# A filter loaded twice by two queues, one product moved to GpSimd, and a shifted schedule in the setup of a fused FFT filter and feed-forward kernel

## The chip, the cores and the metric

The kernel runs on one core of one Trainium2 chip. The metric is device time in microseconds (us), the median of several executions. In this kernel TensorE (PE) multiplies matrices, VectorE (DVE) and ScalarE (ACT) do element-wise work, and GpSimd (POOL) does some of it, more slowly: a two-input operation on 128x512 takes 1.27 us there (L596 on the page of the kernel before) and 0.69 us on VectorE (L591). GpSimd issues DMAs through a software queue (q0 of that page, 13.60 MB), SyncE (SP) through a hardware queue (q1, 73.81 MB), and ScalarE through a hardware queue of its own (q10, 0.13 MB). The page gives the time of all queues as shares of the same 16 DMA engines (10.5%, 32.0% and under 0.1%).

## The reference

```python
# x (8, 3008, 256) f32; filt_r, filt_i (1505, 256); w_in (256, 2048); w_out (2048, 256); beta (2048,)
X = np.fft.rfft(x, axis=1)
y = np.fft.irfft(X * (filt_r + 1j * filt_i)[None], n=3008, axis=1)   # float32
h = y.reshape(-1, 256) @ w_in
out = (h / (1 + np.exp(-beta * h))) @ w_out
```

## The kernel before

The Fourier transform is done as matrix products in four small steps. Batch 0 is transformed in a setup of some 36 us. After that TensorE alternates between feed-forward products (`hps`, `acc`) and the transform steps of the next batch, for all eight batches. In the setup the filters arrive in six units of four rows. A product needs a unit's filter on all 128 partitions, but each DMA fills only 64 of them (`fr` the upper half, `fi` the lower), and GpSimd copies it into the other half:

```python
def load_filters(k0, k1):                     # SyncE: each filter to one half only
    for filt, dst, p0 in ((filt_r, fr_sb, M), (filt_i, fi_sb, 0)):
        for q0, off, sg in ((p0, k0, 1), (p0 + H, N1 - k0, -1)):
            ...
            nc.sync.dma_start(dst[q0 : q0 + H, k0:k1, :], src)

def spread(u):                                # GpSimd: copy to the other half
    nc.gpsimd.tensor_copy(fr_sb[:M, ks, :], fr_sb[M:, ks, :])
    nc.gpsimd.tensor_copy(fi_sb[M:, ks, :], fi_sb[:M, ks, :])

def s2_0(u):                                  # second transform step, times the filter
    ... # four matmuls into ps
    nc.vector.tensor_tensor(pq[u, 0][:], ps[:], fr_sb[:, ks, :], ALU.mult)
    nc.vector.scalar_tensor_tensor(pq[u, 1][:], ps[:], rot[:], fi_sb[:, ks, :], ALU.mult, ALU.mult)

for u in range(4):
    spread(u)
load_win(0, 4 * P)       # GpSimd: 0.26 MB of w_in
spread(4)
load_win(4 * P, FF)      # 0.79 MB of w_in
spread(5)
for g in range(4):
    load_x(1, g)         # GpSimd: xg, the input of batch 1
load_wout(0)             # SyncE: the first half of w_out, two loads of 0.52 MB
load_wout(WG)
scale_wout(0)            # GpSimd
scale_wout(WG)
```

In the trace GpSimd's instructions come in the order of this listing: the copies of unit 3 at 21.32 and 22.41 us, the first part of w_in at 23.40, the copies of unit 4 from 24.29, the second part at 26.37, the copies of unit 5 from 27.14, xg from 29.21, the scaling from 31.34. `unit(u)` is the third transform step of a unit (TensorE, with an evacuation on ScalarE), `a0_turn` transposes, and `spin` is a few matmuls that only keep TensorE busy.

Of the kernel before, what the change touches and what calls it, by code (L numbers as in the profile page):

```python
# [10 lines left out]
P = 128  # L11

ACT = mybir.ActivationFunctionType
ALU = mybir.AluOpType
ENG = mybir.EngineType
F32 = mybir.dt.float32
# [5 lines left out]
N1 = 47  # L22
M = 64
H = M // 2
NK = 24
# [11 lines left out]
def kernel(  # L37
# [10 lines left out]
    nc = tc.nc  # L48

    B, S, D = x.shape  # L50
# [27 lines left out]
    fr_sb = consts.tile([P, NK, D], F32, name="fr_sb", tag="fr_sb")  # L78
    fi_sb = consts.tile([P, NK, D], F32, name="fi_sb", tag="fi_sb")
    KH = 8  # L80
    KU = 4
# [1 line left out]
    WZ = KP * J  # L83
    CH = M * J

    def load_filters(k0, k1):
        n = k1 - k0
        for filt, dst, p0 in ((filt_r, fr_sb, M), (filt_i, fi_sb, 0)):
            for q0, off, sg in ((p0, k0, 1), (p0 + H, N1 - k0, -1)):
                src = AP(filt.tensor, filt.offset + off * D, [[N1 * D, H], [sg * D, n], [1, D]])  # L90
                nc.sync.dma_start(dst[q0 : q0 + H, k0:k1, :], src)  # L91

    t1 = consts.tile([NP, KP], BF16, name="t1", tag="t1")
    t4 = consts.tile([KP, NP], BF16, name="t4", tag="t4")
# [37 lines left out]
    def bank2(shape, dt=F32):  # L132
        return spsum.tile(shape, dt, name="sps", tag="sps")

    def turn8():
        return tpsum.tile([P, KH, P], BF16, name="tps", tag="tps")
# [20 lines left out]
    sr = rpool("setup_a", r_sr, bufs=1)  # L157
# [59 lines left out]
    off = affine("off", c_i, -TURN / 4, TURN / 4)  # L217
# [49 lines left out]
    def spin(n, idle):  # L267
        for _ in range(n):
            nc.tensor.matmul(idle[:], lhsT=rest[:, :P], rhs=rest[:], start=True, stop=True)

    def a0_turn(u, tiles=None, engines=(True,)):
        tiles = tiles or [turn8()]
        n = KU // len(tiles)
        for h, tp in enumerate(tiles):
            for i in range(n):
                k4 = 4 * (u * KU + h * n + i)
                for e in range(NDC):
                    nc.tensor.transpose(
                        tp[:, NDC * i + e, :],
                        aT[:, e, k4 : k4 + 4, :].rearrange("p c j -> p (c j)"),  # L280
                        ident[:],
                    )
        for h, tp in enumerate(tiles):
            k0 = u * KU + h * n
            dst = a0[:, k0 : k0 + n, :].rearrange("p k (e d) -> p (k e) d", e=NDC)
            evac(dst, tp[:, : NDC * n, :], engines[h])
# [7 lines left out]
    def t3_neg(g, on_act):  # L294
        ks = slice(g * KH, (g + 1) * KH)
        evac(t3[:, ks, P:], t3[:, ks, :M], on_act, -1.0)
# [12 lines left out]
    seen = sp.tile([1, 2], BF16, name="seen", tag="seen")  # L309
    nc.sync.dma_start(seen[:], t2[:1, 1, M - 2 : M])  # L310
    for u in range(NUN):
        load_filters(u * KU, (u + 1) * KU)
    gp = nc.gpsimd
    rot = affine("rot", v_i, 2.0, -1.0, gp)
    tiny = sp.tile([P, NFB], F32, name="tiny", tag="tiny")
# [19 lines left out]
    spin(2, idle)  # L335
    s1_0(7, (False, True))
    spin(2, idle)
    a0_turn(0, [turn8(), bank2([P, KH, P], BF16)], (False, True))
    a0_turn(1)
    t3_neg(0, False)  # L340
    nc.vector.reciprocal(rbeta_sb[:], beta_sb[:])

# [14 lines left out]
    WG = 4  # L357
    wstage = {}

    def load_x(b, g):  # L360
        t = xpool.tile([KP, JG, D], BF16, name="xg", tag="xg")
        load_rows(t[:], b, g * JG, (g + 1) * JG)
        xg[b, g] = t
# [9 lines left out]
    def scale_wout(f0):  # L373
        nc.gpsimd.tensor_tensor(
            wout_sb[:, f0 : f0 + WG, :],
            wstage.pop(f0)[:],
            rbeta_sb[:, f0 : f0 + WG].unsqueeze(2).broadcast_to([P, WG, D]),
            ALU.mult,
        )
# [42 lines left out]
    pq = {}  # L422
    r_p0 = ExitStack()
    p0pool = rpool("p0pool", r_p0, bufs=2, **tw)

    def s2_0(u):
        ps = bank2([P, KU, D])
        for i in range(KU):
            k1 = u * KU + i
            nc.tensor.matmul(ps[:, i, :], lhsT=t2[:, k1, :], rhs=a0[:, k1, :], start=True, stop=True)  # L430
        ks = slice(u * KU, (u + 1) * KU)
        for c in range(2):
            pq[u, c] = p0pool.tile([P, KU, D], BF16, name="pq_t", tag=f"pq{c}")
        nc.vector.tensor_tensor(pq[u, 0][:], ps[:], fr_sb[:, ks, :], ALU.mult)
        nc.vector.scalar_tensor_tensor(
            pq[u, 1][:], ps[:], rot[:], fi_sb[:, ks, :], ALU.mult, ALU.mult
        )
# [21 lines left out]
    def unit(u):  # L459
        t = bank2([P, NDC, KU, P])  # L460
        s3_0(u, [t[:, e] for e in range(NDC)])
        ck = KU * P // J
        dst = zT[:].rearrange("p e (j k) -> p e j k", k=KP)
        evac(
            dst[:, :, :, u * ck : (u + 1) * ck],
            t[:].rearrange("p e k (c j) -> p e j (k c)", j=J),
            True,
        )

    def spread(u):  # L470
        ks = slice(u * KU, (u + 1) * KU)
        nc.gpsimd.tensor_copy(fr_sb[:M, ks, :], fr_sb[M:, ks, :])  # L472
        nc.gpsimd.tensor_copy(fi_sb[M:, ks, :], fi_sb[:M, ks, :])  # L473
# [6 lines left out]
    for u in range(4):  # L480
        spread(u)
    load_win(0, 4 * P)
    spread(4)
    load_win(4 * P, FF)
    spread(5)
    for g in range(4):
        load_x(1, g)
    load_wout(0)
    load_wout(WG)
    scale_wout(0)  # L490
    scale_wout(WG)

    s2_0(0)
    a0_turn(2)
# [3 lines left out]
    unit(0)  # L498
    a0_turn(3)
    s2_0(2)  # L500
    unit(1)
    a0_turn(4)
    s2_0(3)
    unit(2)
    s2_0(4)
    a0_turn(5)
    t3_part(2, True)
    t3_neg(2, True)
    unit(3)
    s2_0(5)  # L510
    idle = tpsum.tile([P, 512], F32, name="tps", tag="tps")
    spin(3, idle)
    unit(4)
    banks.close()

# [14 lines left out]
    for e in range(NDC):  # L530
        for h in range(2):
            pool, tag = (lps, "lp") if e else (fps, "fp")
            ps = pool.tile([P, 4, P], F32, name="fp", tag=tag)
# [117 lines left out]
    def at(s, fn, *a):  # L651
        plan.setdefault(int(s), []).append((fn, a))

    def s1_steps(b, units_, steps, act, on_act=()):
        assert len(steps) == len(units_)
        for i, s in zip(units_, steps):
            at(s, s1, b, i, i in on_act)
            if i % 4 == 3:
                at(s, a1_store, b, i // 4)
# [12 lines left out]
    for b in range(1, B):  # L672
        o = first_step[b - 1]
        if b == 1:
            at(0, z_late, 1, 0)
            at(1, z_late, 1, 1)
            s1_steps(1, range(16), [1 + (2 * i + 1) // 3 for i in range(16)], False, (1, 4, 7, 10, 13))
            for i, r in enumerate((11, 12, 13, 14)):
                at(r, f_late, 1, i // 2, i % 2)
            for g in range(NG):  # L680
                at(o + 13, a2_load, 1, g)
            for hh, z0, f0 in ((2, (13, 14), (15, 16, 17, 18)), (3, (18, 19), (20, 21, 22, 23))):
                for e in range(NDC):
                    at(z0[e], z_late, hh, e)
                for i, r in enumerate(f0):
                    at(r, f_late, hh, i // 2, i % 2)
            s23_steps(1, [o + r for r in (22, 24, 26, 28, 30, 34, 36, 38, 40, 42, 44, 46)], 5, 1)
            for h in range(J // JG):
                at(o + 54, zz_load, 1, h)
            s4_steps(1, [o + 66 + (i * 12) // 15 for i in range(16)], 2)  # L690
            for f in (2, 3):
                at(f, load_wout, f * WG)
                at(f, scale_wout, f * WG)
            if B > 2:
                for g in range(4):
                    at(o + 24 + 3 * g, load_x, 2, g)
                late = (54, 55, 56, 57, 58, 59, 60, 61, 66, 67, 68, 70, 72, 73, 74, 76)
                s1_steps(2, range(16), [o + r for r in late], False)
                for g in range(NG):
                    at(o + 80, a2_load, 2, g)  # L700
                if B > 3:
                    for g in range(4):
                        at(o + (62, 68, 88, 92)[g], load_x, 3, g)
            continue
        base = [o + 16 * n + s for n in range(4) for s in (4, 8, 12)]
        if b == 2:
            base[:6] = [o + r for r in (8, 12, 19, 22, 26, 29)]
        s23_steps(b, base, 6, False)
        for h in range(J // JG):
            at(o + 70, zz_load, b, h)  # L710
        s4_steps(b, [o + 80 + (i * 13) // 15 for i in range(16)], False)
        if b + 1 < B:
            early = [o + 16 * n + s for n in range(4) for s in (7, 13)]
            late = [o + s for s in (66, 67, 69, 70, 72, 73, 75, 76)]
            s1_steps(b + 1, range(16), early + late, False)
            for g in range(NG):
                at(o + 82, a2_load, b + 1, g)
            if b + 2 < B:
                for g in range(4):
                    at(o + (30, 62, 88, 92)[g], load_x, b + 2, g)  # L720
# [6 lines left out]
    for s in range(NSTEP):  # L727
        i, fb = divmod(s, NFB)
# [100 lines left out]
```

## Time and profile before

| | before |
|---|---|
| time, median of 3 runs | 782.0 us |
| span of the profiled run | 780.25 us |
| last unit of filters landed | about 26.7 us |
| second part of w_in issued, landed | 26.37, 34.73 us |
| first xg issued, landed | 29.21, 36.56 us |
| first matmul on xg (the rest of the program follows without a wait) | 36.61 us |

The table gives instants from the start of the span, read from the trace's instructions and DMA landings. From the first xg matmul to the end are 780.25 - 36.61 = 743.6 us. The prediction below shows the lines that matter. In them `sps` and `lp` are results of the second and third transform steps, `pq_t` the products with the filters, `y`, `zz`, `zp` and `fp` stages behind them, `ws` w_out as it lands and `wout_sb` the same scaled.

### The profile page before, as it was taken

To read this page: it belongs to the slowest core of one execution; us is meant where nothing else is said; L and a number is where in the kernel's file an instruction comes from. 1 tells how busy PE (TensorE), PEld (TensorE's weight loads), DVE (VectorE), ACT (ScalarE), POOL (GpSimd) and SP (SyncE) were. 2 spreads that over 40 slices of the span, in tenths; PEclk is the share of its full clock that TensorE was granted. 3 is DMA by queue.
4 is the path that set the end of the run, shared out by engine and by line. 5 is a ranking of instruction groups with operands and counts; after the bars stand their busy time and mean duration, and the time that the engine had idled before them with its cause. 6 is when DMAs were issued, how large, how long until landed. Compare 5 with 4: busy or idle time off the path is not lost.

```text
span 780.2 us, 15154 instructions
## 1 busy us (share of the span) xinstructions
PE 764.1 (98%) x5956; PEld 544.0 (70%) x6051; DVE 446.0 (57%) x713; ACT 552.6 (71%) x814; POOL 151.4 (19%) x155
## 2 busy tenths in 40 slices
PE   8899999999999999999999999999999999999997
PEld 5677667766776667866678666776667776676665
DVE  7869754766556665566546665567655666321001
ACT  6767877676677766777667776677766777777776
POOL 6714400312012210122201322022200222000000
PEclk9999999999999999999999999999999999999999
DMA  9975585244913358042671417622164111500101
GB/s 185 233 213 116 147 209 155 70 108 115 252 42 80 103 116 242 29 113 71 152 207 45 119 48 181 176 75 69 48 189 135 48 48 49 156 28 28 55 28 55
DMA packets 84411, 88.51 MB, mean 113 GB/s; under 512 B 5788, under 2 KB 74652, under 8 KB 84340
## 3 DMA queue, kind: packets, MB, share of 16 engines
q1 hardware_dynamic: 79892, 73.81, 32.0%
q0 software_dynamic: 4304, 13.60, 10.5%
q8 instruction: 47, 0.77, 0.4%
q14 instruction: 24, 0.20, 0.1%
q10 hardware_dynamic: 144, 0.13, 0.0%
HBM read 54.47 MB, written 46.66 MB: 130 GB/s over the span
## 4 chain that ended last, share of the span: by engine, by line
PE 94%; DMA 2%; issue 1%; POOL 1%; DVE 1%; SPq 0%; ACT 0%; DVEq 0%; POOLq 0%
PE acc L788 43%; PE hps L770 39%; PE ps L561 3%; PE ps L629 3%; PE ps L607 3%; PE ps L577 2%; DMA xg<-in_x_dram 1%; DMA fi_sb<-in_filt_i_dram 1%; POOL fi_sb L473 0%; POOL fr_sb L472 0%; SPq L91 0%; PE ps L405 0%; PE tp L400 0%; DVE y L114 0%; DVE u L224 0%
## 5 line engine op out<-in xcount | busy, mean ns | idle before, releaser
L779 ACT ACTIVATE gT<-hps,beta_sb 128x512 bf16<-128x512 f32 x752 | 516.9, 687 | 213.3 <-PE hps L770 191.9
L788 PE MATMUL acc<-wout_sb,gT 128*128 128x256 bf16 x3008 | 452.9, 272 | 2.3
L770 PE MATMUL hps<-y,win_sb 128*128 128x512 bf16 (+7 forms) x1636 | 428.0, 350 | 0.1
L788 PEld LDWEIGHTS <-gT 128*128 128x128 bf16 x3008 | 286.9, 98 | 121.6 <-issue 0.9
L596 POOL TENSOR_TENSOR yh<-a_t,b_t 128x512 bf16<-128x512 f32 x84 | 106.4, 1267 | 424.1 <-DVE b_t L595 422.8
L770 PEld LDWEIGHTS <-win_sb 128*128 128x128 bf16 x1728 | 164.8, 98 | 25.2 <-issue 0.9
L112 DVE COPY ost<-acc 128x512 f32<-128x512 f32 (+1 forms) x94 | 59.9, 679 | 138.3 <-PE acc L788 138.2
L112 DVE CAST a<-ps 96x512 bf16<-96x512 f32 x107 | 72.9, 685 | 53.3 <-PE ps L561 49.3
L114 DVE TENSOR_SCALAR y<-ps 128x376 bf16<-128x376 f32 (+2 forms) x128 | 63.3, 510 | 61.2 <-PE ps L629 57.9
L591 DVE TENSOR_TENSOR a_t<-ps,fr_sb 128x512 f32<-128x512 f32 x84 | 58.1, 692 | 67.0 <-PE ps L577 66.5
L592 DVE SCALAR_TENSOR_TENSOR b_t<-ps,fi_sb 64x512 f32<-64x512 f32 x84 | 58.2, 693 | 1.1
L595 DVE TENSOR_TENSOR b_t<-ps,fi_sb 64x512 f32<-64x512 f32 x84 | 57.4, 683 | 1.1
L112 DVE CAST z<-ps 128x512 bf16<-128x512 f32 x72 | 49.3, 684 | 1.7 <-PE ps L607 0.8
L629 PEld LDWEIGHTS <-zz 96*128 96x128 bf16 x448 | 29.7, 97 | 22.9
L561 PE MATMUL ps<-xg,t 94*96 94x512 bf16 x112 | 41.9, 381 | 1.5 <-DMA xg<-in_x_dram 0.8
L629 PE MATMUL ps<-t,zz 96*128 96x94 bf16 x448 | 34.7, 205 | 0.7
L607 PE MATMUL ps<-yh,t 128*128 128x256 bf16 x168 | 32.1, 273 | 0.6
L577 PE MATMUL ps<-a,t 128*128 128x256 bf16 x168 | 32.1, 273 | 0.3
L607 PEld LDWEIGHTS <-t 128*128 128x128 bf16 x168 | 16.2, 98 | 17.7 <-issue 0.7
L577 PEld LDWEIGHTS <-t 128*128 128x128 bf16 x168 | 16.1, 98 | 16.3
L171 POOL DMA_DIRECT2D xg<-in_x_dram x24 | 12.5, 521 | 56.7 <-PE ps L561 56.7
L561 PEld LDWEIGHTS <-t 94*96 94x96 bf16 x112 | 13.8, 123 | 10.3
(95 smaller groups left out, 177.3 us busy)
## 6 DMA issues: line engine op xcount, KB each, us to landing
out_dram<-ost SPq DMA_DIRECT2D x42, 512.0 KB, 3.0
d<-a SPq DMA_DIRECT2D x28, 384.0 KB, 5.1
a<-d SPq DMA_DIRECT2D x28, 384.0 KB, 4.9
d<-z SPq DMA_DIRECT2D x28, 384.0 KB, 3.9
zz<-d SPq DMA_DIRECT2D x28, 384.0 KB, 7.1
xg<-in_x_dram POOLq DMA_DIRECT2D x24, 384.0 KB, 6.3
out_dram<-ost SPq DMA_DIRECT2D x9, 256.0 KB, 3.8
ws<-in_moe_w_out_dram SPq DMA_DIRECT2D x4, 512.0 KB, 6.6
```

What stands on the lines that cost most here:

```text
L112: nc.vector.tensor_copy(dst, src)
L114: nc.vector.tensor_scalar_mul(dst, src, scale)
L561: nc.tensor.matmul(ps[:KP], lhsT=t1[:], rhs=xg[b, g][:NP, jj : jj + 2, :], start=True, stop=True)
L577: nc.tensor.matmul(ps[:, e, :], lhsT=t2[:, k0 + e, :], rhs=st["a2", b, g][:, kk + e, :], start=True, stop=True,)
L591: nc.vector.tensor_tensor(a_t[:], ps[:], fr_sb[:, ks, :], ALU.mult)
L592: nc.vector.scalar_tensor_tensor(b_t[:M], ps[M:], -1.0, fi_sb[M:, ks, :], ALU.mult, ALU.mult)
L596: nc.gpsimd.tensor_tensor(yh[:], a_t[:], b_t[:], ALU.add)
L607: nc.tensor.matmul(ps[:, e, :], lhsT=t3[:, 2 * i + e, :P], rhs=yh[:, e, :], start=True, stop=True)
L629: nc.tensor.matmul(ps[:, e, :NP], lhsT=zz[:, j0 % JG + e, dc * P : (dc + 1) * P], rhs=t4[:], start=True, stop=True,)
L770: nc.tensor.matmul(hps[:, pos - t0 : pos - t0 + ln], lhsT=win_sb[:, dc, fb * P : (fb + 1) * P], rhs=ys[b][:, dc, n0 : n0 + ln], start=(dc ...
L779: nc.scalar.activation(gT[:], hps[:], ACT.Silu, scale=beta_sb[:, fb : fb + 1])
L788: nc.tensor.matmul(acc_of(i, tb)[:, tb % 2, :], lhsT=blk[i * NFB + fb][:, tb * P : (tb + 1) * P], rhs=wout_sb[:, fb, :], start=(fb == 0 an ...
```

## The change

The intent is to free GpSimd, which spends four copies of 1.04 us on the last two units, and with it the issue of w_in and xg. Units 4 and 5 are loaded into both halves, the second time by ScalarE's queue, so that one queue can fill one half while the other fills the other. One of the two products of unit 4 goes to GpSimd, from a copy that ScalarE makes and scales. Transposes and units are reordered, and the first transform of batch 1 starts one step later, with four late pieces of batch 0 moved to steps 2 to 5.

```diff
+    DUP = 2 * KH
+    def load_filter(i, k0, k1, p0, eng):  # one filter, either half, any queue
 ...
     for u in range(NUN):
-        load_filters(u * KU, (u + 1) * KU)
+        for i, p0 in enumerate((M, 0)):
+            load_filter(i, u * KU, (u + 1) * KU, p0, nc.sync)
 ...
+    load_filter(0, DUP, NK, 0, nc.scalar)
     a0_turn(0, ...)
     a0_turn(1)
+    load_filter(1, DUP, NK, M, nc.scalar)
 ...
+        if on_pool:
+            nc.scalar.activation(zc[:], ps[:], ACT.Copy, scale=rot[:])
         nc.vector.tensor_tensor(pq[u, 0][:], ps[:], fr_sb[:, ks, :], ALU.mult)
+        if on_pool:
+            return
 ...
     load_win(0, 4 * P)
-    spread(4)
     load_win(4 * P, FF)
-    spread(5)
-    for g in range(4):
-        load_x(1, g)
+    load_x(1, 0)
+    # pool_product(u): two GpSimd products of 128x512 from zc and fi_sb
 ...
     s2_0(2)
+    a0_turn(4)
     unit(1)
-    a0_turn(4)
     s2_0(3)
+    a0_turn(5)
+    s2_0(4, True)
+    pool_product(4)
+    for g in range(1, 4):
+        load_x(1, g)
+    scale_wout(0)
+    scale_wout(WG)
     unit(2)
 ...                       # unit(3) moves behind s2_0(5) and spin
-            s1_steps(1, range(16), [1 + (2 * i + 1) // 3 ...
-            for i, r in enumerate((11, 12, 13, 14)):
+            s1_steps(1, range(16), [2 + (2 * i + 1) // 3 ...
+            for i, r in enumerate((2, 3, 4, 5)):
                 at(r, f_late, 1, i // 2, i % 2)
```

More of the change, by code (lines that the diff above doesn't have):

```diff
@@ L84 @@
     CH = M * J
-    def load_filters(k0, k1):
-        n = k1 - k0
-        for filt, dst, p0 in ((filt_r, fr_sb, M), (filt_i, fi_sb, 0)):
-            for q0, off, sg in ((p0, k0, 1), (p0 + H, N1 - k0, -1)):
-                src = AP(filt.tensor, filt.offset + off * D, [[N1 * D, H], [sg * D, n], [1, D]])
-                nc.sync.dma_start(dst[q0 : q0 + H, k0:k1, :], src)
+    FILTERS = ((filt_r, fr_sb), (filt_i, fi_sb))
+    DUP = 2 * KH
+    def load_filter(i, k0, k1, p0, eng):
+        filt, dst = FILTERS[i]
+        for q0, off, sg in ((p0, k0, 1), (p0 + H, N1 - k0, -1)):
+            src = AP(filt.tensor, filt.offset + off * D, [[N1 * D, H], [sg * D, k1 - k0], [1, D]])
+            eng.dma_start(dst[q0 : q0 + H, k0:k1, :], src)
     t1 = consts.tile([NP, KP], BF16, name="t1", tag="t1")
@@ L424, with s2_0 @@
     p0pool = rpool("p0pool", r_p0, bufs=2, **tw)
-    def s2_0(u):
+    zc = sr.tile([P, KU, D], F32, name="zc", tag="zc")
+    def s2_0(u, on_pool=False):
         ps = bank2([P, KU, D])
@@ L482, with pool_product @@
     load_win(0, 4 * P)
-    spread(4)
     load_win(4 * P, FF)
-    spread(5)
-    for g in range(4):
-        load_x(1, g)
+    load_x(1, 0)
+    def pool_product(u):
+        for i in range(0, KU, 2):
+            k0 = u * KU + i
+            nc.gpsimd.tensor_tensor(
+                pq[u, 1][:, i : i + 2, :], zc[:, i : i + 2, :], fi_sb[:, k0 : k0 + 2, :], ALU.mult
+            )
     load_wout(0)
     load_wout(WG)
-    scale_wout(0)
-    scale_wout(WG)
     s2_0(0)
@@ L500 @@
     s2_0(2)
+    a0_turn(4)
     unit(1)
-    a0_turn(4)
     s2_0(3)
+    a0_turn(5)
[5 more added lines that the diff above has]
+    scale_wout(WG)
     unit(2)
-    s2_0(4)
-    a0_turn(5)
     t3_part(2, True)
     t3_neg(2, True)
-    unit(3)
     s2_0(5)
@@ L512 @@
     spin(3, idle)
+    unit(3)
     unit(4)
@@ L676 @@
             at(1, z_late, 1, 1)
-            s1_steps(1, range(16), [1 + (2 * i + 1) // 3 for i in range(16)], False, (1, 4, 7, 10, 13))
-            for i, r in enumerate((11, 12, 13, 14)):
+            s1_steps(1, range(16), [2 + (2 * i + 1) // 3 for i in range(16)], False, (1, 4, 7, 10, 13))
+            for i, r in enumerate((2, 3, 4, 5)):
                 at(r, f_late, 1, i // 2, i % 2)
             for g in range(NG):
-                at(o + 13, a2_load, 1, g)
+                at(o + 14, a2_load, 1, g)
             for hh, z0, f0 in ((2, (13, 14), (15, 16, 17, 18)), (3, (18, 19), (20, 21, 22, 23))):
```

## The prediction

> **What bounds the kernel now.** I read the page's busy times, then the waits of TensorE, the chain in order of time, the timelines of the engines and the DMA view by stretch. The page says TensorE is the bound of the whole:
>
> ```profile
> PE 764.1 (98%) x5956; PEld 544.0 (70%) x6051; DVE 446.0 (57%) x713; ACT 552.6 (71%) x814; POOL 151.4 (19%) x155
> ```
>
> The waits of TensorE from 28 us to the end name all that is left to win (us in total, times, longest):
>
> ```profile
> PE sps L444 <- ACT y L110: 1.1, 1, 1.1
> PE ps L561 <- DMA xg<-in_x_dram: 0.8, 1, 0.8
> PE lp L444 <- DVE pq_t L435: 0.6, 1, 0.6
> ```
>
> The reader is to see that nothing is listed after the wait for xg, which ends at 36.61 us: from there to 780.2 us TensorE never waits noticeably. The change leaves TensorE's work as it is. So the end is the start of the first matmul on xg (batch 1's first transform) plus a constant, and the whole question is what happens before 36.6 us. Even a setup of half the length would hardly be 2%.
>
> What sets that start? The chain in order of time, cut to its end (start, us, what):
>
> ```profile
> 22.41 0.93 POOL fi_sb L473
> ...
> 27.14 1.03 POOL fr_sb L472
> ...
> 28.23 0.39 POOL fi_sb L473
> 28.62 0.59 issue
> 29.21 7.35 DMA xg<-in_x_dram
> 36.56 0.04 issue
> 36.61 0.38 PE ps L561
> ```
>
> GpSimd's copies between the halves hold back the issue of xg, and xg then takes 7.35 us. That looks like an order to shorten GpSimd's list. The DMA views of two stretches, 11 to 24.7 us and 25 to 27.5 us, warn against it:
>
> ```profile
> DMA packets 2370, 3.22 MB, mean 235 GB/s; under 512 B 399, under 2 KB 1980, under 8 KB 2369
> DMA packets 795, 0.79 MB, mean 318 GB/s; under 512 B 19, under 2 KB 795, under 8 KB 795
> ```
>
> In both, the busy share of the 16 DMA engines is 9 in nearly every slice; page part 2 shows the same up to about 40 us. First x of batch 0, then 3.1 MB of filters (to 24.8 us), 1.05 MB of w_out, 1.05 MB of w_in and xg stand in one saturated line. xg takes 7.35 us because w_in is ahead of it, not because it was issued late.
>
> The third bound is VectorE's chain of products, one unit per 2.32 us (from its timeline: start, us, engine, line):
>
> ```profile
> 25.38 1.21 DVE L434 TENSOR_TENSOR pq_t<-sps,fr_sb 128x1024 bf16<-128x1024 f32 x1
> 26.52 1.27 DVE L435 SCALAR_TENSOR_TENSOR pq_t<-sps,rot,fi_sb 128x1024 bf16<-128x1024 f32 x1
> 28.20 1.22 DVE L434 TENSOR_TENSOR pq_t<-sps,fr_sb 128x1024 bf16<-128x1024 f32 x1 [0.41 <-POOL fr_sb L472]
> 29.34 1.27 DVE L435 SCALAR_TENSOR_TENSOR pq_t<-sps,rot,fi_sb 128x1024 bf16<-128x1024 f32 x1
> ```
>
> It ends at 30.61; the last unit waited 0.41 us for GpSimd's copy. From there the tail (last unit, turns, fourth transform) leads to the first hps matmul at 33.84.
>
> [...] filters, each to one half, 235 GB/s; w_out, over 128 partitions, 318. [...] from 36.5 to 40 us, with xg on one queue and w_out on the other, they moved 178 and 150 packets. [...] The trace's own row (L596, 128x512 from f32) has 1.27 us, which I use.
>
> **The change part by part.**
>
> GpSimd: four copies of units 4 and 5 go, 4 x 1.04 = 4.2 us. Two products of 128x512 come, 2 x 1.27 = 2.5 us. The w_in loads and the first xg load no longer have copies in between: were fi of unit 3 copied at 23.45 as now, xg's first load would be issued near 25.1 instead of 29.21.
>
> VectorE: one product of unit 4 goes, 1.14 us of its cadence, and with it the 0.41 us of waiting. Without any data wait it would end at 30.61 - 1.55 = 29.1.
>
> ScalarE: four DMA issues, by the SP queue's 0.4 us each 1.6 us, half of them before an evacuation that the first product needs (there ScalarE is idle 0.82 us, so nearly hidden); one scaled copy of 128x1024, 1.02 us; its slack of some 2 us between 21 and 28 us takes it.
>
> TensorE: the first xg matmul moves one step later, behind two more hps matmuls (0.43 us that then lies before the wait): -0.43 us if xg sets the time.
>
> DMA: two filters of 8 rows for 64 partitions, 2 x 64 x 8 x 1 KB = 1.05 MB more, in front of w_in and xg for the most part. Alone at 235 GB/s that is 4.5 us. If the second queue always met the other half, the two would run near the 318 GB/s of w_out or somewhat more. SP's queue changes halves every 262 KB, the ACT queue every 524 KB, so about half of the bytes meet the same half: 1.05 MB of SP's beside 1.05 MB of ACT's is then 1.05/0.36 + 1.05/0.225 = 7.6 us (estimate; 360 for opposite halves, because the fast 1 KB packets of this stretch take the same 46 ns as those of w_out and some are 4 KB) against 4.5 us for SP's alone. Delay of all that follows: 3.1 us. [...]
>
> So the last filters land near 26.7 + 3.1 = 29.8 us instead of about 26.7 (the next-to-last landing is at 26.1): the last product starts at about 29.8 and not at 28.0, and ends near 31.1. The products on GpSimd end near 30, so the fifth unit's second half and its evacuation come about when the last unit's do. The setup then ends 0.2 to 0.5 us later than now, in place of 1.5 earlier: the copies' time is given back as transfer time.
>
> xg: 36.56 + 3.1 for the filters, less what is taken from w_out, which now shares the DMA engines packet for packet with an earlier w_in: 250 to 2000 ns, say 1.2. That gives 38.5. The matmul starts 38.5 - 36.6 = 1.9 us later; less 0.43 makes +1.5 us.
>
> **The rivals.**
>
> A, the intended course: [...] the 1.05 MB cost only about 1 us; the setup ends 1 us or more earlier, w_in starts at 25.5 and xg lands at 36 or before. For it: most 4 KB filter packets take about 290 ns, a few 159[...]; and the moved steps (transform at step 2, four late pieces at steps 2 to 5) look fitted to a measured course. Against it: xg can't land before all the filters, w_in and itself have moved. It makes -1.5 to 0 us.
>
> B, full collision: the queues serialize [...], w_in isn't brought forward because GpSimd's copies of unit 3 wait for late filters, and the product on GpSimd comes last. For it: the saturated DMA row. It makes +2.5 to +4 us.
>
> C, a new wait after the first steps: w_out's first groups come later, and their scaling on GpSimd, now behind the products and three xg issues, must be ready for the first acc matmul (37.7 us now; scaling ended near 33.2, so 4.5 us of slack). I expect no wait, at most 1 us.
>
> **Range and chances.** My middle course says +1.5, A about -0.8, B +3. With weights 0.45, 0.4 and 0.15 the mean is 0.675 - 0.32 + 0.45 = +0.8; from 782.0 I choose 782.7. The range holds A whole and most of B: 780.3 to 785.2. 2% is 15.6 us, a good part of the whole setup of 36 us, so either side gets 0.01.
>
> **What would show each step right or wrong.** Right: a DMA queue of 1.05 MB on ScalarE; the throughput between 17 and 25 us only somewhat above 235 GB/s (260 to 300); VectorE's last product waits for a DMA and not for a copy; the one wait of TensorE after 33 us is for xg, longer than 0.84 us, ending at 37.5 to 39; no wait later. Wrong: a throughput of 350 or more there (A), a last product that ends before 30 us, xg's matmul at 36 us or earlier; or waits of acc for w_out's scaling (C). My prediction would fail most of all by a misjudged rate of two queues to two halves.

The forecast's own sum: 36.56 + 3.1 - 1.2 = 38.5 us for xg, 1.9 us later, less 0.43 makes +1.5; with A at -0.8 and B at +3, weighted, it is +0.8, and 782.7 us was chosen. Two of its terms are estimates. The 3.1 comes from 360 GB/s for opposite halves (1 KB in 46 ns on each of 16 DMA engines are 356 GB/s) and 225 for the same half (near the 226 of the filters from 16 to 22 us); that opposite halves would run faster was inferred from 235 GB/s for filters and 318 for w_out. The 1.2, out of 250 to 2000 ns, has no working beside it but the 178 and 150 packets. B's +2.5 to +4 us is an estimate too.

## The result

The changed kernel takes **786.94 us** (786.05 to 787.72, 4 runs) against 782.19 us (781.81 to 782.61, 4 runs) for the kernel before in the same rounds. The ratio is 1.006, with a 95% interval of 1.0043 to 1.0078: within 2%, but slower by 4.75 us, and above the predicted range. All ratios here are the mean time of one kernel's fast runs over that of the other's of the same rounds, so they are not quite the ratio of the quoted medians.

| us from the start of the span | before | after |
|---|---|---|
| first of the third unit's two fr loads landed | 18.26 | 23.56 |
| last filter landed | about 26.7 | 31.63 |
| two parts of w_in issued | 23.40, 26.37 | 28.62, 29.45 |
| second part of w_in landed | 34.73 | 39.97 |
| first xg issued, landed | 29.21, 36.56 | 30.17, 41.88 |
| first hps matmul | 33.84 | 39.48 |
| first xg matmul | 36.61 | 41.92 |
| from there to the end | 743.64 | 742.93 |
| span | 780.25 | 784.85 |

The span grew by 4.60 us: 5.31 us later at the first xg matmul, less 0.71 us in the rest. The page of the changed kernel shows the same busy time of TensorE, and a new hardware queue (number: packets, MB, share):

```profile
PE 764.9 (97%) x5955; PEld 545.0 (69%) x6051; DVE 445.4 (57%) x712; ACT 553.6 (71%) x815; POOL 149.8 (19%) x153
...
q10 hardware_dynamic: 784, 1.18, 0.7%
```

Queue 10 is ScalarE's. It moved 0.13 MB before, so 1.05 MB came on. These are the waits of TensorE from 24 us to the end (total us, times, longest):

```profile
PE sps L437 <- DVE pq_t L446: 4.3, 1, 4.3
PE sps L455 <- ACT y L112: 1.1, 1, 1.1
PE zp L405 <- ACT y L112: 0.4, 1, 0.4
PE sps L437 <- ACT y L112: 0.3, 1, 0.3
```

The wait for xg is gone from the list (0.09 us is left of it), and no wait follows. That doesn't mean that xg is no longer late. The setup itself now ends at about 41.83 us, in the same instant in which xg lands. Two chains, one through the filters and one through w_in, have both moved by some 5 us. The chain in order of time (start, us, what):

```profile
13.59 5.83 DMA fr_sb<-in_filt_r_dram
...
19.43 0.32 SPq L93
...
24.30 1.04 POOL fr_sb L483
...
29.45 0.71 POOL win_sb L487
30.17 11.71 DMA xg<-in_x_dram
41.88 0.04 issue
41.92 0.38 PE ps L580
```

xg now takes 11.71 us from issue to landing, in place of 7.35. At the head of the chain stands a transfer of ScalarE's, for which SyncE waited until 19.43. The line of transfers from 11 to 24.7 us was as full as before and no faster; the same view of before, in the prediction, has 3.22 MB at 235 GB/s:

```profile
DMA packets 2078, 3.08 MB, mean 225 GB/s; under 512 B 318, under 2 KB 1732, under 8 KB 2013
...
q1 hardware_dynamic: 1393, 1.96, 62.7%
q10 hardware_dynamic: 640, 1.05, 37.6%
```

So ScalarE's 1.05 MB (q10) came in place of SyncE's bytes (q1), and not beside them. The timeline of GpSimd shows whom that held (start, us, line, operation; in brackets the idle time and its releaser):

```profile
24.30 1.04 POOL L483 COPY fr_sb<-fr_sb 64x1024 f32<-64x1024 f32 x1 [4.80 <-DMA fr_sb<-in_filt_r_dram]
...
28.62 1.57 POOL L487 DMA_DIRECT2D win_sb<-in_moe_w_in_dram  x2
...
30.80 2.50 POOL L500 TENSOR_TENSOR pq_t<-zc,fi_sb 128x512 bf16<-128x512 f32 x2
```

GpSimd had no more copies for units 4 and 5, but it waited 4.80 us for the third unit, and so it issued w_in 5.2 us later than before instead of earlier. VectorE shows the same stall, and an end at 35.64 us instead of 30.61:

```profile
25.37 1.22 DVE L443 TENSOR_TENSOR pq_t<-sps,fr_sb 128x1024 bf16<-128x1024 f32 x1 [3.77 <-POOL fr_sb L483]
...
33.22 1.22 DVE L443 TENSOR_TENSOR pq_t<-sps,fr_sb 128x1024 bf16<-128x1024 f32 x1 [1.97 <-PE sps L455]
34.36 1.27 DVE L446 SCALAR_TENSOR_TENSOR pq_t<-sps,rot,fi_sb 128x1024 bf16<-128x1024 f32 x1
```

TensorE's own clock fell as well. The granted clock is the share of its full speed at which TensorE was allowed to run. Two rows of the stretches from 28 to 32 us (the columns are named under `e1` below; the third from the end is the clock):

```profile
28.00:30.00 2.00, 2.00 (x21) 1.97 (x20) 2.00 (x2) 1.11 (x1) 2.00 (x3) 0.59 1.06 217
30.00:32.00 2.00, 1.74 (x14) 1.40 (x13) 1.25 (x2) 1.83 (x2) 1.94 (x3) 0.55 0.94 290
```

This came after TensorE's wait of 4.27 us, which ended at 27.85, and it made the setup's own work slower, just before VectorE's last unit, which waited 1.97 us for TensorE: four matmuls of the second step took 0.84 us at 31.25, and 0.60 at 22.54 under the full clock. What this alone added to the setup no run isolates. The time as a whole doesn't show it, since xg landed no earlier than the setup ended.

Why ScalarE's bytes went first: SyncE issued nothing between 13.64 us and 19.43 us, when ScalarE's first load had landed (19.42). The profile lists 5.8 us of that as SyncE's queue waiting for the load (`fr_sb<-in_filt_r_dram`). Why SyncE's next load had to wait for it, the trace doesn't show.

Two theories follow. **Bytes:** the 1.05 MB stand in front of everything, and cost their own length whoever loads them. **Stall:** the loss comes from SyncE's halt and the order that it makes. A further rival says that it comes from what the change does to the engines.

### The profile page after: what moved, and what is told of

The parts are those of the page before. It is cut to its first block, busy times and chain, and to the rows that moved or that the text cites. A ratio compares the mean times of both kernels' runs of the same rounds, so it can differ in the third digit from the quotient of the medians.

```text
span 784.8 us, 15152 instructions
## 1 busy us (share of the span) xinstructions
PE 764.9 (97%) x5955; PEld 545.0 (69%) x6051; DVE 445.4 (57%) x712; ACT 553.6 (71%) x815; POOL 149.8 (19%) x153
## 4 chain that ended last, share of the span: by engine, by line
PE 93%; DMA 3%; POOL 1%; issue 1%; DVE 1%; ACT 1%; DVEq 0%; SPq 0%; POOLq 0%
PE acc L807 43%; PE hps L789 39%; PE ps L580 3%; PE ps L648 3%; PE ps L626 3%; PE ps L596 2%; DMA xg<-in_x_dram 1%; DMA fr_sb<-in_filt_r_dram 1%; PE ps L410 0%; ACT aT L112 0%; POOL fi_sb L484 0%; POOL fr_sb L483 0%; PE tp L405 0%; DVE u L226 0%; DVE u L147 0%
```

## The experiments

Eleven of the twelve runs test the loss and its parts, and the twelfth tries for a better version. Each ran beside the kernel before, with medians of 782.49 us for the first four, 782.46 us for the next four, 782.07 us for `e9` and `e11`, and 782.6 us for `e10` and `e12`.

| run | what | median (range) us | ratio to before, 95% | first xg landed | first xg matmul |
|---|---|---|---|---|---|
| e1_loads_alone | before + double loads - copies | 788.43 (787.56–789.47) | 1.0072 (1.0057–1.0087) | 42.58 | 42.62 |
| e2_rest_alone | after without double loads and GpSimd product | 781.37 (781.09–781.79) | 0.9982 (0.9967–0.9997) | 37.05 | 37.09 |
| e3_one_queue | after, all loads on SyncE | 791.96 (791.10–793.63) | 1.0113 (1.0096–1.0130) | 38.85 | 49.20 |
| e4_act_later | after, ScalarE issues later | 792.22 (791.76–792.60) | 1.0120 (1.0105–1.0135) | 37.93 | 47.25 |
| e5_held | e3, w_in held behind the filters | 786.95 (786.21–787.86) | 1.0055 (1.0038–1.0072) | 41.83 | 41.87 |
| e6_half_loads | e1, only unit 5 doubled | 786.47 (785.15–788.63) | 1.0049 (1.0029–1.0070) | 40.32 | 40.37 |
| e7_rest_product | e2 + the GpSimd product | 783.98 (783.05–785.64) | 1.0017 (1.0002–1.0032) | 36.24 | 39.50 |
| e8_wout_late | e2, second w_out load behind xg | 781.08 (780.34–782.26) | 0.9981 (0.9964–0.9997) | 35.66 | 36.11 |
| e9_held_wout | e5, second w_out load behind xg | 786.50 (785.23–786.91) | 1.0053 (1.0037–1.0070) | 41.02 | 41.77 |
| e10_tighter | e8, two small moves | 782.15 (781.89–782.60) | 0.9996 (0.9983–1.0010) | 36.86 | 36.90 |
| e11_bytes | e2 + 1.05 MB that nothing reads, early | 792.06 (789.48–792.65) | 1.0123 (1.0105–1.0140) | 40.45 | 40.49 |
| e12_bytes_late | e2 + the same bytes at 56 us | 781.13 (780.87–781.52) | 0.9983 (0.9969–0.9996) | 36.69 | 36.74 |

### The change split in two: e1_loads_alone and e2_rest_alone

```diff
 # e1: the kernel before, with
+    load_filter(0, DUP, NK, 0, nc.scalar)   # around a0_turn(0), a0_turn(1)
+    load_filter(1, DUP, NK, M, nc.scalar)
-    spread(4)
-    spread(5)
 # e2: the changed kernel, with
-    load_filter(0, DUP, NK, 0, nc.scalar)
-    load_filter(1, DUP, NK, M, nc.scalar)
+    spread(4)                               # around load_win, as before
+    spread(5)
-    s2_0(4, True)
-    pool_product(4)
+    s2_0(4)
```

> The kernel before with one part of the change alone: units 4 and 5 loaded to both halves, the second copy by ScalarE's queue, GpSimd's four copies gone; product, order and schedule as before. Theory S ([...] SyncE's third unit is issued only when ScalarE's first load has landed, and all 1.05 MB go ahead of it): the whole loss is here, 786 to 787.5 us, SyncE's load of the third unit issued at about 19.4 us, VectorE waiting over 3 us for unit 2. Rival V (the bytes cost the same wherever they stand): also 786 to 787.5. Rival P (the loss comes from the product on GpSimd, the order and the schedule): 782 to 784.

> The changed kernel without the second copy of the loads: GpSimd copies units 4 and 5 again and VectorE makes both products; the order of turns, of the x loads and the schedule of batch 1 as changed. Theory S and rival V: about as before, 781.3 to 782.5 us, the first xg landing near 36.6 us and its matmul one step later. Rival P: 784 us or more.

The double loads alone cost 5.9 us: all of the loss and more. The reordering and the shifted schedule alone gain 1.1 us, and that kernel is faster than both. The first xg landed at 42.58 us in `e1`. Its longest wait after 30 us, and its row for 42.9 to 46.3 us (stretch; its length; busy us and instructions of PE, PEld, DVE, ACT and POOL; granted clock; DMA share; GB/s):

```profile
PE ps L564 <- DMA xg<-in_x_dram: 2.5, 1, 2.5
```

```profile
42.90:46.30 3.40, 3.40 (x12) 1.66 (x11) 1.37 (x2) 1.17 (x2) 0.00 (x0) 0.51 1.07 230
```

After a wait of 2.53 us the clock stood at 0.51 for 3.4 us. That is why the rest took 745.07 us in `e1` and not 743.64: late transfers cost twice, once as a wait and once as some 1.5 us at half clock. In `e2` the rest took 742.60 us, so the schedule part of the change does what it was made for.

### Stall or bytes: e3_one_queue, e4_act_later, e5_held

```diff
 # e3: the changed kernel, with the second halves on SyncE, each right behind its first
             load_filter(i, u * KU, (u + 1) * KU, p0, nc.sync)
+            if u * KU >= DUP:
+                load_filter(i, u * KU, (u + 1) * KU, M - p0, nc.sync)
 ...                                       # and no load_filter on nc.scalar
 # e4: the changed kernel, with ScalarE's issues behind a0_turn(2) and unit(0)
 # e5: e3, and GpSimd reads one column of unit 4's fi before it issues w_in
+    gp.tensor_copy(hold[:], fi_sb[:, DUP + KU - 1, :1])
     load_win(0, 4 * P)
```

> The changed kernel with the same 1.05 MB loaded by SyncE's queue, each unit's second half right behind its first, ScalarE issuing none. Theory S: units 0 to 3 land as in the kernel before (third unit's fr near 18.9 us), VectorE doesn't stall before unit 2, w_in is issued near 23.4 us; what is left is the later last units: 783.3 to 785 us. Rival V: as the changed kernel, 786.5 to 787.5 us.

> The changed kernel with ScalarE's four issues moved behind the evacuation of the third turn and of unit 0, some 2 to 5 us later. Theory S: SyncE's third unit is issued before ScalarE's loads fill the engines, unit 2's stall of VectorE (3.8 us) shrinks to under 2 us: 783.5 to 786 us. Rival V: as the changed kernel, 786.5 to 787.5 us.

> The single-queue kernel of the run before, with one small GpSimd copy that reads unit 4's fi (both halves) in front of the issue of w_in, so that w_in and xg can't be taken before most filters have landed. Theory T (there is one saturated line of transfers: w_in's and xg's long packets, alternating with the filters' short ones, starve whatever filters are still in line): the last filter lands at about 32 us instead of 38 to 40, VectorE's last product starts at 32 to 33 instead of 40.9, and the time falls from 792.0 to 784.0 to 786.0 us. Rival V (the bytes alone cost it, the order of the line doesn't matter): stays at 791 to 792.5.

The stall theory fell with `e3` and `e5`. `e3` takes the stall away and was expected faster than the changed kernel, but it is 5 us slower still. `e4` was meant to take it away too, but only moves it: SyncE issued nothing from 19.09 to 25.63 us, until another load of ScalarE's had landed (25.62). So `e4`, as slow as `e3`, says nothing for or against the theory. xg came early in both (38.85 and 37.93 us), yet the setup ended late. (In `e3` xg landed before the last filter, so the prediction's "xg can't land before all the filters" doesn't hold there.) From VectorE's timeline of `e3`:

```profile
32.20 1.23 DVE L443 TENSOR_TENSOR pq_t<-sps,fr_sb 128x1024 bf16<-128x1024 f32 x1 [5.28 <-DMA fr_sb<-in_filt_r_dram]
40.93 1.28 DVE L446 SCALAR_TENSOR_TENSOR pq_t<-sps,rot,fi_sb 128x1024 bf16<-128x1024 f32 x1 [7.51 <-DMA fi_sb<-in_filt_i_dram]
```

GpSimd, no longer held, issued w_in at 24.21 us, and from then on w_in and xg shared the DMA engines with the filters, for which VectorE waited 5.28 and 7.51 us. That their packets alternated is the author's reading of `e3`; the counts at hand are of other loads (178 and 150 packets of two queues in the kernel before, 417 and 412 in `e11`). The last filter landed at about 40.6 us (VectorE's wait for it ends at 40.93) instead of 31.63. Part of what `e3` and `e4` lose is the clock: it was 0.50 from 32.8 to 46.4 us in `e3` and from 33.8 to 43.9 us in `e4`. In the changed kernel, it seems, the stall had by accident kept w_in behind the filters. `e5` does so on purpose, without any load on ScalarE. Its VectorE keeps the cadence of before until 26 us, and it has the same time as the changed kernel (786.95 and 786.94 us) and the same landing of xg (41.83 and 41.88 us). So the loss needs neither ScalarE's queue nor the stall.

`e4` also shows the two queues at work together, from 17 to 21 us:

```profile
DMA packets 588, 0.92 MB, mean 231 GB/s; under 512 B 79, under 2 KB 500, under 8 KB 556
...
q10 hardware_dynamic: 303, 0.51, 52.2%
q1 hardware_dynamic: 285, 0.41, 46.2%
```

Two queues filled filters at once, with about as many packets each, at 231 GB/s in sum. Their halves were opposite for a part of this time only, since SyncE changes halves with every filter and unit. One queue alone has 226 GB/s from 16 to 22 us in the kernel before, and 236 in `e5`. So the two queues, in the order that this kernel gives them, gained nothing. A rate for opposite halves alone, without this mixing, no run here isolates.

### Half the bytes: e6_half_loads

```diff
-    DUP = 2 * KH
+    DUP = 5 * KU            # only unit 5 is loaded twice
 ...
     load_win(0, 4 * P)
+    spread(4)
```

> As the loads alone, but unit 5 only is loaded to both halves (0.52 MB instead of 1.05) and GpSimd copies unit 4 again. Theory T: the line of transfers moves by half as much, xg lands at 39 to 40 us, 784.5 to 786.3 us. Rival Q (the damage is SyncE's queue waiting [...], whatever the size): like the loads alone, 787.5 to 788.5.

With 0.52 MB more, xg landed 3.76 us later than before, and with 1.05 MB (`e1`) 6.02 us. The delay grows with the bytes, though not quite in proportion. The rest took 745.29 us, after a wait of 2.72 us and in an execution with a mean clock of 0.997. The four executions show what slow stretches cost: the two with a mean clock of 1.000 took 785.15 and 785.51 us, the two with 0.997 took 787.43 and 788.63 us.

### The bytes by themselves: e11_bytes and e12_bytes_late

```diff
 # e11: e2, and behind SyncE's filter units
+    for i, p0 in ((0, 0), (1, M)):
+        for q0, off, sg in ((p0, DUP, 1), (p0 + H, N1 - DUP, -1)):
+            ...
+            nc.sync.dma_start(unused[q0 : q0 + H], src)
 # e12: e2, and the same rows, in two parts of four rows, at a later step
+            at(o + 15, load_unused)
```

> This is e2_rest_alone (no double load, all products on VectorE, 781.4 us) with the same 1.05 MB of filter rows loaded by SyncE behind the units into a tile that nothing reads. No copy is taken away, ScalarE issues no load, nothing waits for these bytes. Theory (the bytes alone make the loss): xg lands at 41.5 to 42.3 us instead of 37.05, TensorE waits some 5 us for it and runs at half clock for some 3.4 us after the wait, 786 to 788.5 us. Rival (the loss comes from what the double load does to the engines: the copies that are gone, the ScalarE queue[...]): 781.4 to 782.5 us.

> This is e2_rest_alone with the same 1.05 MB of filter rows as in e11_bytes, loaded by SyncE too, into tiles that nothing reads, but at about 56 us, after the first xg and all w_out loads, where no stage waits for the line at once. Theory (the bytes cost because they stand in the line in front of w_in, xg and w_out): the first xg lands at 36.5 to 37.5 us as in e2_rest_alone and the time is 781.0 to 782.2 us, within 0.8 us of e2_rest_alone. Rival (the bytes or the number of DMAs cost wherever they are): 785 us or more.

`e11` settles that the bytes suffice: no copy was removed, ScalarE issued nothing, nothing waits for them, and the kernel lost 10.7 us against `e2`. Its size was not as expected, since two waits came where one had been foreseen. TensorE's waits from 30 us, and two rows of the DMA view from 36 to 44 us:

```profile
PE acc L811 <- POOL wout_sb L383: 4.8, 1, 4.8
PE ps L584 <- DMA xg<-in_x_dram: 4.3, 1, 4.3
```

```profile
q0 software_dynamic: 417, 1.42, 88.2%
q1 hardware_dynamic: 412, 0.41, 18.0%
```

In `e2` the first two loads of w_out run nearly alone, at 333 GB/s between 25.5 and 28 us (812 packets of q1 to 6 of w_in's software queue). In `e11` the extra bytes take that gap, and w_out (1 KB packets on q1) then shares the DMA engines packet for packet with w_in and xg (3 and 4 KB on q0): as many packets, but 0.41 against 1.42 MB. xg was late by 3.4 us instead of about 5, since w_out had in effect stepped behind it. The first part of w_out landed at 44.11 us, and TensorE waited 4.83 us more for it. With the clock at half from 39.8 to 50.0 us, the rest took 750.14 us.

`e12` moves the same bytes to some 56 us, where no stage is about to run dry. It takes 781.13 us, as `e2` does. So neither the volume nor the number of DMAs costs anything by itself. The bytes cost because of what stands behind them in the line.

### The product on GpSimd: e7_rest_product

```diff
 # e2, with
-    s2_0(4)
+    s2_0(4, True)
+    pool_product(4)
```

> The changed kernel with only the second copy of the loads undone: GpSimd copies units 4 and 5 again and also makes the product of unit 4. Beside the run with the rest alone it tells what the product on GpSimd does. GpSimd now has 2.5 us more in front of the later x loads; the product ends near 32.3 us, 2 us after the last product on VectorE, so the fifth unit closes the setup about 1.5 us later, but xg is waited for anyway: 781.5 to 783.5 us. If the product helped, as intended, it would be under 781.3.

This part is slower too, by 2.6 us against `e2`. From TensorE's waits between 24 and 60 us:

```profile
PE sps L453 <- POOL pq_t L500: 2.0, 2, 1.1
```

xg was there at 36.24 us, but the setup only let TensorE take it at 39.50. The two products last 1.26 us each, as predicted, but they start at 29.48 us, when GpSimd is done with its other work, and the third step of unit 4 waits for them. Not all of the 2.6 us are these waits: the clock was 0.50 from 32.4 to 35.7 us, and the one execution with a mean clock of 1.000 took 783.05 us, 1.7 us more than `e2`. In the changed kernel the same cost lies under the wait for late transfers.

### What bounds e2 and e5 next: e8_wout_late, e9_held_wout, e10_tighter

```diff
 # e8: e2, with
-    load_wout(WG)
 ...
+    load_wout(WG, nc.gpsimd)     # behind the first xg load
     for g in range(1, 4):
         load_x(1, g)
 # e9: e5, with the same move
 # e10: e8, without spin(3) before unit(3), and
+    nc.gpsimd.tensor_copy(fr_sb[:M, 5 * KU :, :], fr_sb[M:, 5 * KU :, :])
     load_win(4 * P, FF)          # the copy was behind this issue
```

> The rest alone (781.4 us), with the second w_out load (0.52 MB) taken out of SyncE's line and issued by GpSimd behind the first xg load. Theory T: xg lands 0.8 to 1.6 us earlier (35.5 to 36.3 us), TensorE's wait for it of 0.83 us goes, 780.2 to 781.0 us; the accumulating matmuls of the fifth group must not wait for the later scaling. If the setup and not the line of transfers were the bound: no change, 781.2 to 781.8.

> This is e5_held with the second w_out load (0.52 MB) taken from in front of the first xg and issued behind it. Theory (bytes in front of xg at some 220 to 235 GB/s set the end): xg lands some 1.6 us earlier than the 41.83 us of e5_held, about 40.2 us, and the time is about 785.3 us (784.8 to 786.0). Rival (what is in front doesn't matter, xg or the setup is late from something else): xg lands at 41.5 to 42 us and the time stays at 786.5 to 787.5 us.

> This is e8_wout_late (781.1 us) without the three spin matmuls in front of unit 3 and with the fr copy of unit 5 issued in front of the second part of w_in. With xg there in time (35.7 us), the setup sets the end, so each tenth of a microsecond taken from it should show in the span: TensorE starts on the first xg at 35.5 to 36.0 us instead of 36.1, and the time is 780.5 to 781.1 us. If the end is set by something else still, 781.0 to 781.5 us.

`e8` takes xg's wait away: it lands at 35.66 us, and after 34 us no wait of TensorE is listed. The time is 781.08 us, the lowest median of all, though no more than 0.3 us below `e2`, which the ranges don't resolve. The setup ends at the same point.

`e9` missed. xg landed 0.8 us earlier than in `e5` and not 1.6, and the first xg matmul hardly moved (41.77 us), because the setup was now the later one. Its row for 33.1 to 39.4 us, and that of `e5` for 32.9 to 36.3 us:

```profile
33.10:39.40 6.30, 5.13 (x48) 4.21 (x47) 4.21 (x11) 3.53 (x7) 3.50 (x5) 0.50 1.08 230
```

```profile
32.90:36.30 3.40, 3.40 (x35) 3.13 (x33) 1.93 (x5) 2.27 (x4) 1.32 (x3) 0.50 1.10 269
```

Both ran at half clock after the waits for late filters and for GpSimd's product, `e5` for 3.4 us and `e9` for about 6.8 us (its row from 39 to 40 us still has 0.56). So `e9` doesn't test the bytes in front of xg cleanly: the clock seems to have taken back what the shorter line gave. Why the clock stayed low for twice as long I did not settle. The slow stretches read in these runs lasted 3.4 us (the changed kernel, 28.37 to 31.78 us, `e1` and `e5`), 6.8 (`e9`), 10.2 (`e11`) and 13.6 (`e3`). Nor do the runs show which waits bring one on. In `e1` one followed a wait of 2.53 us. In `e7` no wait of TensorE from 24 to 60 us was over 1.1 us, and yet the clock fell (0.50 from 32.4 to 35.7 us); in the kernel before (from 11 us on) and in `e2` (20 to 45 us) the longest was 1.1 us too, and the clock was 1.00 (4.7 to 779.6 us before, 12 to 44 us in `e2`). `e9` had another wait of 0.64 us at 34.26, and its last filter landed some 0.7 us later.

`e10` missed as well, and shows how thin the margin is. The copy put in front of the issue of w_in's second part delayed that issue by 1.2 us (26.45 to 27.65 us), and xg landed 1.2 us later (35.66 to 36.86). The `spin` that was dropped at the same time isn't told apart from this. TensorE's waits from 30 us:

```profile
PE acc L805 <- POOL wout_sb L377: 0.6, 1, 0.6
PE ps L578 <- DMA xg<-in_x_dram: 0.6, 1, 0.6
```

## Why the prediction was wrong

**Right.** The frame held in every run without a late second wait or a slow clock after the first xg matmul: span = first xg matmul + a constant. It is 743.6 us with the old schedule and 742.6 to 743.1 with the new one, which is the predicted 0.43 us and a little more. The warning held that GpSimd's shorter list gives nothing while the line in front is full, though `e10` shows that the list counts too: 1.2 us in front of w_in came out as 1.2 us at xg. GpSimd's product took 1.27 us for each 128x512, as predicted from its other row. The class (within 2%) was right as well.

**The step that failed: "Delay of all that follows: 3.1 us".** It was worked out as 7.6 us of mixed loading against 4.5 us, with 360 GB/s assumed for half of the bytes, those that meet the opposite half. The measured delay was 4.9 to 5.3 us: third unit 5.3, last filter about 4.9, w_in 5.2, xg 5.3. No stretch of filters shows such a rate: two queues together moved 231 GB/s in `e4`, and 1.05 MB at the measured 206 to 225 GB/s of the changed kernel are 4.7 to 5.1 us. My evidence for 360 was the 46 ns of the fast 1 KB packets, which are as short as w_out's over 128 partitions; but they were only the fastest of the filters' packets. In the trace of the kernel before the filters' 1 KB packets take 67 ns (median, 16 to 22 us), and the 1 KB packets while w_out loads 48 ns (26 to 28 us).

**The second step: "less what is taken from w_out ... say 1.2".** Nothing was taken back. It needed an earlier w_in, and so a GpSimd that is free. But GpSimd's remaining copies waited for filters that the double load had delayed, so w_in was issued at 28.62 us and not at 23.40. The prediction's line "xg's first load would be issued near 25.1" fell for the same reason (30.17). Together, 5.3 in place of 3.1 - 1.2 = 1.9 us account for the miss of the middle course (+1.5 us foreseen, +4.6 in the span): the schedule's gain (0.71 us) hardly differs from the 0.43 assumed.

**"The setup then ends 0.2 to 0.5 us later"** was off by more: the first hps matmul came 5.64 us later. I had added the delay to the last filter's landing and then let the removed copies offset most of it. The last product was to end near 31.1 us and ended at 35.64. (The 28.0 us that the prediction gives for the start of the last product now is in no line of its timeline, which has 28.20 and 29.34.) ScalarE's issues were not nearly hidden either: the second took 1.67 us, and VectorE's first product began at 16.86 us instead of 16.08; the longer stall covered that. Rival B named most of this course (queues serialize, w_in not brought forward), but at +2.5 to +4 us and a weight of 0.15 it was both too small and too lightly weighted. The product on GpSimd did not come last, as B has it: it ended at 33.30 us, before VectorE's. B also missed that ScalarE's megabyte would go ahead of units 2 to 5. `e5` shows that this order is not what sets the end.

**Of the signs named beforehand:** ScalarE's queue of 1.05 MB appeared. The throughput from 17 to 25 us was 218 GB/s, below the 260 to 300 named. VectorE's last unit waited for TensorE, which had run at half clock until 31.8 us, and not for a DMA. The wait for xg vanished instead of growing, as the setup was as late as xg. Rival C, a wait for w_out's scaling, did not come in the changed kernel; it came in `e10` (0.6 us) and in `e11` (4.83 us), where w_out landed later.

**Where the expected gain went.** The removed copies did save GpSimd's time, but in the changed kernel GpSimd spent more than that waiting for late filters (4.80 us). What the saved time would be worth without the added bytes no run shows. The shifted schedule did gain, 1.1 us with the reordering (`e2`). The product on GpSimd costs 2.6 us where transfers are in time (`e7`, 1.7 without the slow clock), and the bytes in front of w_in, w_out and xg cost more than either (5.9 us in `e1`). How the parts add up inside the changed kernel, where one hides another, stays open: loads alone (+5.9) and rest alone (-1.1) happen to add to its +4.75, but `e1` contains some 1.5 us of half clock after the first xg wait that the changed kernel doesn't have.

## What to carry to other kernels

Before loading something twice to save a copy, look at whether the transfer line is full at that place. If it is, as here, the copy on an engine with time to spare can be the cheaper one, and a byte costs what stands behind it in the line (nothing for 1.05 MB at 56 us, 10.7 us for the same bytes at 25 us). An engine's duty to issue DMAs makes its waits for data the waits of every later transfer (GpSimd's 4.80 us for a filter, and w_in issued 5.2 us later, in the changed kernel); and where queues shared the DMA engines packet for packet (`e11`, 417 and 412 packets in 8 us), the one with the larger packets got most of the bandwidth (1.42 MB against 0.41). The best kernels keep the copies, and take from the change only the reordering and the schedule (781.1 to 781.4 us against 782.5).
